# An attention and spectral-mix kernel with some 290 TensorE instructions fewer: the last unit of modes as rows, two batches' last rows side by side, one transpose for v's last keys

## The chip, the cores and the metric

The kernel runs on one core of a Trainium2 chip. The metric is the device time of one execution in microseconds (us), the median of several runs. PE is the matrix engine (TensorE), PEld its weight loads, DVE the vector engine, ACT the scalar engine, POOL the GpSimd engine, which here also issues nearly all loads, and SP the engine that issues the stores. Sixteen DMA engines move the data.

## The reference

```python
def _attn_ref(q, k, v, f):            # 8 batches, 8 heads, 576 rows, 64 columns
    scores = scale * np.matmul(q, k.transpose(0, 1, 3, 2))
    cum = np.cumsum(np.log(np.clip(f, 0.0001, 1.0)), axis=-1)
    decay = cum[:, :, :, None] - cum[:, :, None, :]
    scores = np.where(causal, -1e9, scores + decay)
    attn = np.exp(scores - np.max(scores, axis=-1, keepdims=True))
    attn = attn / (np.sum(attn, axis=-1, keepdims=True) + 1e-09)
    return np.matmul(attn, v)

def _moe_ref(x, w_r, w_i, w_ch):      # x: 8 x 576 x 512; w_r, w_i: 64 x 512 x 512
    X = np.fft.rfft(x, axis=1)
    Y[:, :64] = X[:, :64] times (w_r + 1j * w_i), mode by mode (512 x 512 each)
    u = x + np.fft.irfft(Y, n=S, axis=1)
    return u + np.maximum(u @ w_ch, 0.0)
```

The attention's output, its heads side by side, is the x of the second part. The weights w_r and w_i are 134 MB of float32, read once; they are turned into bf16 on their way in.

## The kernel before, in words

The program is written out in a fixed order for every engine: there is no scheduler.

The attention is a loop of 34 turns over 32 pairs of heads (`pairs`, four head pairs for each of eight batches). Turn i computes the scores and exponentials of pair i (`scores`), the product with v of pair i-1 (`av`, `norm`) and the Fourier modes of pair i-2 (`dft`), and turns q and k of pair i+1 (`trans`). v passes through `scale_v`, `turn_v` (eighteen 64 x 64 transposes into `tv`, then a DVE copy into `vT`) and `back_v` (transposes of vT into `vp`: four of 128 keys, and two of 64 for the last 64 keys, one for each head; then an ACT copy into `vs`). A sequence of 576 rows is five blocks, four of 128 and one of 64 (`SBLK`). At the head of a turn POOL issues the loads of q and k for pair i+4 (L112), of v for pair i+3 (L122), and one or two half tiles of weights (`issue_half`, L167, L176, L185). From turn 10 on, weight tiles that have come in are used at once (`spec_early`).

A weight tile holds a quarter (`dc`, 0 to 3) of a unit `u` of four modes: 1 MB in bf16. There are 16 units, so 64 tiles, in seven buffers and some guests' places. `spec_mms` multiplies a tile as 8 matmuls of 512 columns, the modes of all batches as the small operand; the result is rows of modes in `A`. `spec_cols` does it the other way round, 32 matmuls of 16 columns with the weights as the stationary operand, which gives columns, `AT`, that need no turning. Before the change the last unit (u = 15) is done by `spec_cols` in all its quarters and summed in `accT`. The last tile (15, 3) comes in four pieces, one for each mode.

After the attention, a loop over the units takes the tiles as they come. `Yb` adds the early sums, `to_rows` turns rows into columns (`yps`, into `YT` or `YLa`). Beside this, `xw` multiplies a batch's x by w_ch (XW), and from unit 12 on `folds` adds the first twelve units' modes to x and XW: `fold_modes` once for a batch, then `fold_u` and `fold_z` for each block of rows. `SHARE` sets how much of it lies between two weight tiles; what is left is done ahead of (15, 2). Within (15, 2) and (15, 3) stand `base_mm` calls that start the output's first banks (U0, Z0, U1); those with `stop=True` are repeated later and only keep PE at work.

The tail begins when the last piece is used: six DVE sums put the last modes into `YLa` and `YLw`, `last_modes` turns them, and 18 steps write two blocks of 128 x 512 each (`rest`, `copy_u`, o_sb, out_dram).

## Time and profile before

| | |
|---|---|
| median of 3 runs | 435.96 us (435.72 to 436.53) |
| profiled execution, its own time | 436.07 us |
| its span in the profile | 434.2 us |
| busy, share of the span | PE 83%, DVE 61%, ACT 53%, POOL 32% |
| PE instructions, matmuls and weight loads | 4433 and 4444 |
| moved by DMA | 96.79 MB, 223 GB/s over the span |

The profile is of one execution; times are microseconds from the start of its span. L12 is line 12 of the kernel. A group's row says: line, engine, operation, output from input with its shape, count, busy time, and how long its engine stood idle ahead of it and for what. The page's line GB/s has the span in 40 slices of 10.9 us. In a table of stretches the columns are the stretch, its length, the busy time of PE, PEld, DVE, ACT and POOL with the number of instructions, the granted PE clock, the share of the sixteen DMA engines that is busy (it can pass 1, as packets overlap) and GB/s. The queue q0 carries the loads that POOL issues, q1 SP's transfers, q8 and q14 the engines' instructions.

### The profile page before, as it was taken

The numbers are of one execution on the slowest core, as the hardware profiler recorded it, in microseconds if no ns is written. First come the engines' busy times: TensorE is split into PE (matmuls) and PEld (weight loads), VectorE is DVE, ScalarE is ACT, GpSimd is POOL, SyncE is SP. The second block draws the span as 40 slices with busy tenths as digits, with TensorE's granted clock in tenths as the row PEclk, the third lists the DMA queues.
The fourth block names the chain that finished last, engine by engine and source line by source line (L and its number), as shares of the span: only waits on it lengthen the run. The fifth ranks groups of instructions, "written<-read, shape, count | busy, mean of one in ns | idle before, by whom it ended". The sixth has DMA issues, their size and how long they took to land.

```text
span 434.2 us, 10695 instructions
## 1 busy us (share of the span) xinstructions
PE 360.4 (83%) x4433; PEld 200.9 (46%) x4444; DVE 265.7 (61%) x651; ACT 229.0 (53%) x374; POOL 141.0 (32%) x211
## 2 busy tenths in 40 slices
PE   1699999988898899999986386599788599989993
PEld 1466666655665565665653133244343233334330
DVE  6687888776878797787785122222323157654794
ACT  4656667677775567667661022033313176652783
POOL 6544445434544434444304101111111112001273
PEclk9999999999999999999999579599969699999997
DMA  9999999999999999999999999999999999996598
GB/s 193 205 234 220 232 222 232 226 229 230 231 231 228 230 230 230 230 230 229 236 214 212 212 212 212 212 213 212 212 212 212 212 212 212 211 212 126 188 381 305
DMA packets 60289, 96.79 MB, mean 223 GB/s; under 512 B 3664, under 2 KB 28752, under 8 KB 60240
## 3 DMA queue, kind: packets, MB, share of 16 engines
q0 software_dynamic: 54544, 85.63, 103.6%
q1 hardware_dynamic: 5696, 10.47, 6.7%
q8 instruction: 35, 0.57, 0.5%
q14 instruction: 14, 0.11, 0.1%
HBM read 163.73 MB, written 9.44 MB: 399 GB/s over the span
## 4 chain that ended last, share of the span: by engine, by line
DMA 49%; PE 31%; DVE 9%; ACT 5%; issue 3%; POOL 1%; DVEq 0%; ACTq 0%; POOLq 0%
DMA w<-in_moe_w_i_dram 34%; DMA w<-in_moe_w_r_dram 13%; PE pd L536 5%; PE pav L505 5%; PE sps L457 5%; DVE qkT L382 4%; PE tv L404 3%; ACT et L464 2%; PE A L221 2%; PE pd L557 2%; DVE vT L406 2%; PE tp L377 2%; DMA qk<-in_k_dram 2%; DVE x_all L520 2%; PE U L692 2%
## 5 line engine op out<-in xcount | busy, mean ns | idle before, releaser
L464 ACT ACTIVATE et<-sps 128x1024 bf16<-128x1024 f32 x96 | 93.2, 1023 | 11.6 <-PE sps L457 9.7
L505 PE MATMUL pav<-vs,et 128*128 128x65 bf16 (+1 forms) x896 | 51.3, 197 | 14.6 <-ACT e L451 14.3
L505 PEld LDWEIGHTS <-et 128*128 128x128 bf16 (+1 forms) x896 | 39.9, 103 | 34.0 <-issue 31.7
L382 DVE COPY qkT<-tp 128x640 bf16<-128x640 bf16 x64 | 48.9, 765 | 3.4 <-PE tp L377 3.4
L892 DVE TENSOR_TENSOR Yb<-A,yx 128x512 bf16<-128x512 f32 x15 | 10.4, 692 | 59.0 <-PE A L221 59.0
L406 DVE COPY vT<-tv 128x576 bf16<-128x576 bf16 x32 | 24.2, 757 | 35.4 <-PE tv L404 34.7
L732 PE MATMUL pxw<-wch,xT 128*128 128x512 bf16 (+1 forms) x152 | 41.1, 418 | 1.0 <-DVE xT L722 0.4
L457 PE MATMUL sps<-qkT 64*128 64x512 bf16 (+4 forms) x320 | 39.4, 310 | 1.3 <-DVE qkT L382 1.1
L426 ACT COPY vs<-vp 128x576 bf16<-128x576 bf16 x32 | 20.4, 639 | 37.1 <-PE vp L422 37.1
L520 DVE TENSOR_TENSOR x_all<-pav,rcp 128x384 bf16<-128x384 f32 (+2 forms) x96 | 36.2, 377 | 3.3
L221 PE MATMUL A<-w,XP 128*16 128x512 bf16 (+1 forms) x240 | 21.3, 435 | 20.2 <-DMA w<-in_moe_w_i_dram 12.1
L377 PE MATMUL tp<-ident_bf,qk 128*64 128x128 bf16 x576 | 30.1, 235 | 9.3 <-DMA qk<-in_k_dram 9.0
L185 POOL DMA_DIRECT2D w<-in_moe_w_r_dram x16 | 11.9, 743 | 74.6 <-PE A L221 69.2
L739 ACT CAST XW<-pxw 128x512 bf16<-128x512 f32 (+1 forms) x16 | 9.4, 585 | 45.2 <-PE pxw L732 45.2
L739 ACT CAST yx<-pxw 128x512 bf16<-128x512 f32 (+1 forms) x24 | 14.0, 585 | 33.9 <-PE pxw L732 33.9
L782 ACT CAST x_all<-pu 128x512 bf16<-128x512 f32 (+1 forms) x40 | 23.4, 585 | 13.1 <-PE pu L775 12.2
L112 POOL DMA_DIRECT2D qk<-in_q_dram x32 | 19.5, 609 | 30.8 <-PE tp L377 6.5
L185 POOL DMA_DIRECT2D w<-in_moe_w_i_dram x19 | 13.3, 698 | 50.0 <-PE A L221 40.5
L732 PEld LDWEIGHTS <-xT 128*128 128x128 bf16 (+1 forms) x160 | 15.8, 109 | 22.9 <-issue 9.6
L722 DVE COPY xT<-ptr 128x576 bf16<-128x576 bf16 x32 | 14.7, 458 | 17.8 <-PE ptr L717 17.0
L112 POOL DMA_DIRECT2D qk<-in_k_dram x32 | 19.2, 601 | 19.1 <-DMA w<-in_moe_w_i_dram 5.9
L377 PEld LDWEIGHTS <-qk 128*64 128x64 bf16 x576 | 19.5, 116 | 12.7 <-issue 8.2
(158 smaller groups left out, 703.3 us busy)
## 6 DMA issues: line engine op xcount, KB each, us to landing
w<-in_moe_w_i_dram POOLq DMA_DIRECT2D x19, 1024.0 KB, 31.9
w<-in_moe_w_r_dram POOLq DMA_DIRECT2D x16, 1024.0 KB, 29.9
w<-in_moe_w_r_dram POOLq DMA_DIRECT2D x23, 512.0 KB, 11.3
w<-in_moe_w_i_dram POOLq DMA_DIRECT2D x19, 512.0 KB, 11.0
out_dram<-o_sb SPq DMA_DIRECT2D x36, 256.0 KB, 2.8
vt<-in_v_dram POOLq DMA_DIRECT2D x29, 288.0 KB, 10.4
qk<-in_q_dram POOLq DMA_DIRECT2D x32, 144.0 KB, 10.7
qk<-in_k_dram POOLq DMA_DIRECT2D x32, 144.0 KB, 10.7
```

The lines of the kernel that those rows point to most:

```text
L112: nc.gpsimd.dma_start(qk[64 * n : 64 * n + 64, :, :], src[b, 2 * g : 2 * g + 2, :, :].rearrange("h (p r) d -> p h (r d)", p=64),)
L185: nc.gpsimd.dma_start(w8[:, j : j + step, :, :].rearrange("p m r e -> p m (r e)"), src[m : m + step, 256:512, :].rearrange("m (p r) e -> p ...
L221: nc.tensor.matmul(A[32 * j : 32 * j + M, :], lhsT=lhsT, rhs=rhs, start=st_, stop=sp_)
L377: nc.tensor.transpose(tp[64 * hp : 64 * hp + 64, r - r0, :, :].rearrange("p n c -> p (n c)"), qk[:, hp, r * 64 : r * 64 + 64], ident_bf[:, :],
L382: nc.vector.tensor_copy(st[i]["T"][:].rearrange("p n (c r) -> p n c r", r=9)[:, :, :, r0:r1], tp[:, 0 : r1 - r0, :, :].rearrange("p r n c ...
L406: nc.vector.tensor_copy(st[i]["vT"][:].rearrange("p (c r) -> p c r", r=9), tv[:].rearrange("p r c -> p c r"))
L457: nc.tensor.matmul(ps[:, hp, c : c + n], lhsT=KT[sl, jb * 128 : jb * 128 + 128], rhs=QT[sl, i0 : i0 + n], start=True, stop=True,)
L464: nc.scalar.activation(st[i]["et"][:, T, :, :], ps[:], ACT.Exp, scale=scale)
L505: nc.tensor.matmul(pav[:Ms, sb % 3, hp, :], lhsT=eblk(i, hp, jb, sb), rhs=rhs, start=(jb == 0), stop=(jb == sb),)
L520: nc.vector.tensor_tensor(x_all[:ns, g, b, lo:hi, :].rearrange("p s (h d) -> p s h d", h=2), pav[:ns, lo % 3 : lo % 3 + n, :, 0:Dh], _stri ...
L732: nc.tensor.matmul(pxw[rows, :], lhsT=xT[:, eb, sb * 128 : sb * 128 + Ms], rhs=wch[:, eb, :], start=(eb == 0), stop=(eb == NEB - 1),)
L739: nc.scalar.copy(XW[to][rows, sb, :], pxw[rows, :])
```

## The change

1. The last unit's first three quarters are done by `spec_mms` as rows, as those of the other units are: (15, 0) in the attention, (15, 1) and (15, 2) into one bank A. A float32 sum `Yf` is turned by four float32 matmuls (`ypf`, with `perm_f`) and copied into `accT` between the first and the second piece of the last tile.
2. Z0 is started ahead of (15, 2), U0 between the second and third piece, each once; the repeated `base_mm` calls for U0 and Z0 are gone. U1's stay.
3. The 64 last rows of two batches share one block of 128 partitions of `x_all` (`place`). `xw` treats them as one block for each two batches, and `folds` too.
4. v's last 64 keys are doubled by a POOL copy behind vT, so that one transpose of 128 turns them for both heads; `vs` and `wT` have ten places for nine, and `setup_w` two activations for four.
5. `e4` has one buffer for two. `SHARE` is 19.1 for 19.8.

In the instruction lists PE has 8568 rows for 8862, DVE 643 for 647, ACT 363 for 373, and POOL has 32 copies more.

```diff
@@ turn_v, back_v @@
-        st[i]["vT"] = vTpool.tile([128, S], BF16, tag="vT", name="vT")
+        st[i]["vT"] = vTpool.tile([128, S + 64], BF16, tag="vT", name="vT")
...
+        nc.gpsimd.tensor_copy(st[i]["vT"][:, S : S + 64], st[i]["vT"][:, S - 64 : S])
...
-        for jb in range(4):
+        for jb in range(NSB):
             nc.tensor.transpose(
                 vp[:, 2 * jb : 2 * jb + 2, :].rearrange("p h d -> p (h d)"),
                 vT[:, jb * 128 : jb * 128 + 128],
                 ident_bf[:, :],
             )
-        for hp in range(2):
-            sl = slice(64 * hp, 64 * hp + 64)
-            nc.tensor.transpose(vp[sl, 8, :], vT[sl, 512:576], ident_bf[sl, sl])
@@ spec_early @@
-        if u == NU - 1:
-            AT = psM.tile([128, NEB, 8, B], F32, tag="m", name="AT0")
-            spec_cols(AT, dc)
-            nc.vector.tensor_copy(accT[:], AT[:].rearrange("p e c b -> p e b c"))
-            return
@@ xw @@
+                blocks = [(b, sc) for sc in range(NSB - 1)] + ([(b - 1, NSB - 1)] if b % 2 else [])
...
-                for sb in range(NSB):
+                for to, sb in blocks:
@@ folds @@
+            def modes_to(ps, b, sb, which, start):
+                for c in (b, b + 1) if sb == NSB - 1 else (b,):
+                    rows, _ = place(c, sb)
+                    nc.tensor.matmul(
+                        ps[rows, :],
+                        lhsT=BI[:KF, sb * 128 : sb * 128 + SBLK[sb]],
+                        rhs=ys[c][which][:KF, :],
+                        start=start,
+                        stop=True,
+                    )
...
-            SHARE = 19.8
-            work = [(b, sb) for b in range(B) for sb in range(-1, NSB)]
+            SHARE = 19.1
+            work = [(b, sb) for b in range(B) for sb in range(-1, NSB - 1)]
+            for p in range(B // 2):
+                work.insert(11 * p + 10, (2 * p, NSB - 1))
@@ the last unit @@
                     if last and dc == NEB - 2:
-                        U0 = [bank(psT, "U0") for _ in range(2)]
-                        for n in range(4):
-                            base_mm(U0[n % 2], 0, n % 2, 0, True)
+                        L0 = [bank(psX, "pyl"), bank(psX, "pywl")]
+                        Z0 = [bank(psX, "Z0") for _ in range(2)]
+                        for k in range(2):
+                            base_mm(Z0[k], 0, k, 1)
...
                         if dc < NEB - 1:
-                            spec_cols(AT, dc)
-                            nc.vector.tensor_tensor(
-                                accT[:], AT[:].rearrange("p e c b -> p e b c"), accT[:], ALU.add
-                            )
+                            spec_mms(A, u, dc, dc == 1, dc == 2)
+                            if dc == 2:
+                                Yf = xtp.tile([128, D], F32, tag="yf", name="Yf")
+                                nc.vector.tensor_tensor(Yf[:], A[:], yacc[u // 2][:, u % 2, :], ALU.add)
                         else:
+                            AT = psA.tile([128, NEB, 8, B], F32, tag="a", name="AT1")
                             for j in range(4):
                                 if j == 1:
-                                    for stop in (True, False):
-                                        for k in range(2):
-                                            base_mm(U0[k], 0, k, 0, stop)
+                                    ypf = bank(psT, "ypf")[:, 0 : 64 * NEB].rearrange(
+                                        "p (e c) -> p e c", e=NEB
+                                    )
+                                    for eb in range(NEB):
+                                        nc.tensor.matmul(
+                                            ypf[:, eb, :],
+                                            lhsT=Yf[:, eb * 128 : (eb + 1) * 128],
+                                            rhs=perm_f[:],
+                                            start=True,
+                                            stop=True,
+                                        )
+                                    nc.vector.tensor_copy(
+                                        accT[:], ypf.rearrange("p e (b c) -> p e b c", b=B)
+                                    )
                                 elif j == 2:
-                                    L0 = [bank(psX, "pyl"), bank(psX, "pywl")]
-                                    Z0 = [bank(psX, "Z0") for _ in range(2)]
-                                    for stop in (True, False):
-                                        for k in range(2):
-                                            base_mm(Z0[k], 0, k, 1, stop)
+                                    U0 = [bank(psT, "U0") for _ in range(2)]
+                                    for k in range(2):
+                                        base_mm(U0[k], 0, k, 0)
```

## The prediction

> **What bounds the kernel now.** I read the page first, then the chain that ended last, then the stretch around the last weights, and last the DMA packets themselves. The page:
>
> ```profile
> GB/s 193 205 234 220 232 222 232 226 229 230 231 231 228 230 230 230 230 230 229 236 214 212 212 212 212 212 213 212 212 212 212 212 212 212 211 212 126 188 381 305
> q8 instruction: 35, 0.57, 0.5%
> DMA 49%; PE 31%; DVE 9%; ACT 5%; issue 3%; POOL 1%; DVEq 0%; ACTq 0%; POOLq 0%
> ```
>
> The transfers run at an even 230, then 212 GB/s until slice 36: the weights never stop coming, though PE is at half clock or idle in places. The chain in order of time, from 360 us on:
>
> ```profile
> 375.92 25.61 DMA w<-in_moe_w_i_dram
> 401.58 0.40 PE AT L233 x8
> ```
>
> From 189 us to 401.5 the chain is the weight stream; the rest (401.6 to 434.2) is the tail that computes and writes the output. The timeline around the seam:
>
> ```profile
> 390.55 1.01 PEld L233 LDWEIGHTS <-w 128*128 128x128 bf16 x32 [0.68 <-DMA w<-in_moe_w_i_dram]
> 394.89 1.04 PE L692 MATMUL U<-x_all,ident_il 128*128 128x512 bf16 x4
> 396.56 0.97 PEld L233 LDWEIGHTS <-w 128*128 128x128 bf16 x32 [1.13 <-DMA w<-in_moe_w_r_dram]
> ...
> 401.58 0.28 PEld L233 LDWEIGHTS <-w 128*128 128x128 bf16 x8 [0.65 <-DMA w<-in_moe_w_i_dram]
> ...
> 402.02 0.29 DVE L880 TENSOR_TENSOR YLa<-AT,accT 128x128 bf16<-128x128 f32 x1 [3.91 <-PE AT L233]
> ```
>
> PE waits for every piece of the last unit and starts 0.04 us after it lands. So PE work taken out ahead of 401.5 us gives nothing by itself. But look at the DMA share (last but one column) in the last microseconds of that stream:
>
> ```profile
> 392.00:394.00 2.00, 2.00 (x10) 0.75 (x8) 1.75 (x4) 1.71 (x3) 0.12 (x1) 1.00 1.13 211
> 395.00:396.00 1.00, 0.92 (x4) 0.20 (x2) 0.97 (x2) 0.00 (x0) 0.00 (x0) 1.00 0.68 127
> 398.00:399.00 1.00, 1.00 (x12) 0.35 (x8) 0.11 (x1) 0.00 (x0) 0.00 (x0) 1.00 0.55 102
> 400.00:401.00 1.00, 0.98 (x11) 0.44 (x11) 0.00 (x0) 0.00 (x0) 0.00 (x0) 1.00 0.08 14
> ```
>
> The share falls to a half, then to one engine of sixteen (0.08): the engines don't finish together, and the last one alone holds the kernel. Each transfer leaves sixteen landings in the trace, one per DMA engine. Of the last transfer they stand at 394.48 us (first), six more by 395.8, then 398.3, seven from 398.9 to 399.8, and 401.54. The laggard's distance to the first engine grew in steps: 1.6 us at 25 us, 2.2 at 80, 3.6 at 95, 4.8 at 158, 5.9 at 227, 6.0 still at 384.5 (landings 384.53 to 390.51), 7.1 at 389.5. The steps lie at the packets of queue q8, PE's own instructions (16 KB, 256 instructions, each 0.89 to 1.09 us): numbers 0, 8, 16, 24 and 32 of that queue start at 22.6, 89.4, 155.5, 220.4 and 390.9 us. While one runs, 1.07 fewer data packets are in flight (mean of 30). So these packets go round eight engines, and every eighth stops the laggard for about 1.1 us.
>
> **The change part by part.**
>
> The end of the weights. Number 32, at 390.94 us, is the term. PE had then started 8411 of the trace's 8931 PE records. The instruction lists of the two kernels have 8862 and 8568 rows; four of the added ones are f32 matmuls with a weight load each, so about 290 records go and some 8641 stay. A packet is asked for at a fixed count from the program's start, number 32 near 8384 to 8411 (PE stood at 8384 at its wait before 390.55; number 33, 256 later, came with 8653 started, which gives 8397). In the new program that is 257 to 230 from the end, while the last unit's last weight matmul is 297 from the end, counted in the list. So packet 32 now comes some 40 to 67 PE instructions after the last weight is used, and PE cannot run ahead past its wait for that weight. Number 31 moves to about 388 us, on another engine whose distance (5.3 us) does not lead. The laggard stays at 6.0: last landing 401.54 - 1.06 = 400.48 us. Gain 1.06 us; bounds 0 (the packet still falls ahead) and 1.1.
>
> Is PE ready 1.06 us earlier? The third quarter (15, 2) would land at 395.46 instead of 396.52. Ahead of it: (15, 1) in eight matmuls of 512 columns (0.65 us by the A row, for 1.13), the last folds (12 matmuls for 13; the old ones took 391.5 to 394.95, 0.27 each, so 391.15 to 394.4), the DVE adds that free PSUM for Z0 (1.2 us after PE's last, as before: 395.6) and two Z0 matmuls (0.43): 396.2, so 0.7 us late. Then 0.65 for (15, 2), 0.15 and 0.69 for the DVE sum Yf (the Yb row), four f32 matmuls of 64 columns (0.72 by the cpn row), the second piece (0.40), the DVE copy to accT (0.42), which the second U0 bank waits for, and 0.43 for U0. That ends near 399.6; the third piece and three fillers (0.40, 0.65) bring PE to 400.65, 0.17 us after the last landing. I take 0.15 late; bounds 0 and 0.5. The six deleted filler matmuls (1.04 us at 394.9, 0.4 more later) had lain in waits.
>
> The tail. From the last piece on the list is the same, instruction by instruction, so it shifts whole. One thing changes: packet 34 (422.5 us) puts one engine 1.7 us behind during the output, and its last output still lands at 433.25 where the next engine is 0.4 ahead. The new program is shorter than number 33's count (8640 to 8667, against 8641), so probably no such packet is left: between 0 and -0.55 us, I take -0.3.
>
> The early part. Per turn of the attention loop one transpose fewer (six took 0.60 us, five about 0.5), and (15, 0) in 8 matmuls instead of 32 (0.66 for 1.13): all under the DMA stream, nothing. What is added is a GpSimd copy of 64 columns (the nearest row, YLw 128x192, takes 0.35 us). It stands in GpSimd's queue behind the turn's DMA issues, and PE's back_v waits for it. One turn of before:
>
> ```profile
> 81.94 0.40 PE L415 MATMUL vp<-ident_bf,vT 128*128 128x128 bf16 x4
> ...
> 84.62 0.56 POOL L122 DMA_DIRECT2D vt<-in_v_dram  x1 [2.01 <-DVE vn L394]
> 85.17 0.75 POOL L167 DMA_DIRECT2D w<-in_moe_w_i_dram  x1
> ```
>
> GpSimd would reach this copy at 85.9 us, 4.0 after PE wants it; the same sum is 2.5 at turn 4, 4.0 at turn 9, 4.1 at turn 27. So PE, and DVE behind it, falls 4.3 us back in the attention and stays there, as PE is busy over 85% of it. That is a real new wait, and I cost it at nothing, since PE idles from 237.7 to 241.9 for weights that come at their own pace. GpSimd's issues, in turn, now wait for DVE's vT where PE is the late one: up to 2.6 us at turns 18 to 20, and 5 to 6.5 us at 215 to 229. At those points 1.7 MB, and after the delays 0.9 MB, are still queued: 7.5 and 4.2 us at 225 and 212 GB/s. The stream does not break. If that cover is gone, each microsecond of gap is one of the total.
>
> The rest (setup, one fewer turn of 64 rows per batch pair, 36 for 40 XW matmuls, SHARE) is PE and ACT work under the same stream: nothing.
>
> Two rules of the Trainium skill touch this. The row: PE's clock was halved after windows of 3.4 us with PE busy 0.28 and 0.45 of them, and not after one of 0.53. By "TensorE: Matmul & The Clock Gate" (Part 1) one idle window of about 3.4 us halves the clock, which speaks against taking fillers out. In my schedule PE is busy some 0.75 of 391 to 400.5, so neither row nor rule halves it; it is a rival below. "Runtime: NRT & Kernel Launch" (Instruction fetch mechanics) has blocks of 256 instructions, as the 16 KB packets show, and calls their cost mostly hidden. By that the count of instructions would be worth nothing and the time would stay at 435.9; the landings speak against it.
>
> Sum against the profiled execution (436.07 us, span 434.2): -1.06 + 0.15 - 0.3 = -1.21, so 434.86; the median of the runs is 0.11 lower: **434.8 us**.
>
> **The rivals.**
> - *No gain* (same): packet 32 still meets the laggard, the round goes over other engines, or PE is later than 0.5 us. Against it: the count from the end. For it: the count is known to some 20 instructions and PE's margin is thin. Time 435.5 to 436.0. A halved clock at 397 to 400 us belongs here: the f32 matmuls, pieces and U0 would take about 0.8 us more, 435.6.
> - *GpSimd's queue starves the stream* (slower): copy, vT and issues form one loop. For it: the 4.3 us above. It costs from the point where PE's slip passes 8.7 us (4.3 plus the 4.4 us that 0.9 MB lasts at 212 GB/s); at 11 us the stream stands 2.3 us and the time is 437.1, more at each later turn. Against it: GpSimd idles about 2 us at most issues for a free DMA place, which takes up short delays.
> - *The change does not do what it says*: the lists show 294 PE rows fewer, so no chance for this.
>
> **How the numbers follow.** A measurement of this kernel can tell about 0.2%, 0.87 us. Forecast case 0.60, all of it faster by more than that unless both small terms go wrong; no gain 0.26; starved stream 0.14. The range for 8 in 10: low 434.2 (both small terms at their best, run scatter 0.2), high 436.4 (no gain, plus the 0.5 by which the runs of before scatter upward); the starved stream is left out. The likeliest case alone: 434.2 to 435.2.
>
> **What would show it.** Right: the landings of the last transfer end 6.0 us after the first, the last piece starts near 400.5, q8 has 34 packets or fewer and none between 389 and 400.5; back_v waits for POOL by up to 4 us in the attention; the GB/s line keeps 230 and 212. Wrong: a q8 packet between 390 and 400 with the distance again near 7; the last piece starting well after its landing; or a dip in the GB/s line near 155 or 230 us.

## The result: slower by a quarter of a per cent, and the profile after

The changed kernel takes 436.77 us (median of 17 runs, 435.88 to 437.96) where the kernel before took 435.68 (17 runs, 434.89 to 436.77) on the same chip: 1.0025 times, with a 95% interval of 1.0015 to 1.0035. Forecast was 434.8 (434.2 to 436.4). A second measurement of the same kernel, e5 below, gave 1.0011 [0.9996, 1.0025]. One execution there, a slow one of 545.22 us, is left out of the ratio. The profiled execution took 437.01 us, its span is 435.2 (1.0 more than before).

The lines of its page that answer to those of before:

```profile
GB/s 188 205 235 219 233 220 232 228 226 232 231 230 228 230 229 231 229 231 229 236 214 207 212 212 211 212 212 212 212 212 212 212 212 212 212 211 112 211 382 280
q8 instruction: 34, 0.56, 0.5%
DMA 51%; PE 25%; issue 8%; DVE 6%; POOL 5%; ACT 3%; DVEq 0%; POOLq 0%; ACTq 0%
```

q8 has 34 packets, as forecast. The GB/s line has one small dip, 207 in the 22nd slice (228.5 to 239.4 us). The chain, from 371 us on:

```profile
371.56 28.23 DMA w<-in_moe_w_i_dram
400.26 1.28 PE U L691 x3
401.77 0.85 PE U L691 x2
```

The weight stream still carries it to the tail, but now the chain enters PE through the filler matmuls (U, L691) and not through the last piece of the last weight. The timeline around the seam says why:

```profile
396.05 0.64 PE L221 MATMUL A<-w,XP 128*16 128x512 bf16 x8 [1.11 <-DMA w<-in_moe_w_r_dram]
397.27 0.41 PE L233 MATMUL AT<-XP,w 128*128 128x16 bf16 x8 [0.57 <-DMA w<-in_moe_w_i_dram]
397.52 1.08 PE L849 MATMUL ypf<-perm_f,Yf 128*128 128x64 f32 x8
398.52 0.42 PE L233 MATMUL AT<-XP,w 128*128 128x16 bf16 x8
398.78 0.72 PE L691 MATMUL U<-x_all,ident_il 128*128 128x512 bf16 x2
399.84 0.42 PE L233 MATMUL AT<-XP,w 128*128 128x16 bf16 x8 [0.34 <-DMA w<-in_moe_w_i_dram]
400.10 1.44 PE L691 MATMUL U<-x_all,ident_bf 128*128 128x512 bf16 x3
401.33 0.44 PE L233 MATMUL AT<-XP,w 128*128 128x16 bf16 x8
```

The last transfer's sixteen landings now run from 395.21 to 401.03 us (before: 394.48 to 401.54). The last piece could start at 401.07 and starts at 401.33, behind three fillers that took 1.44 us. The same fillers in the kernel before:

```profile
400.61 0.81 PE L692 MATMUL U<-x_all,ident_bf 128*128 128x512 bf16 x3
401.58 0.40 PE L233 MATMUL AT<-XP,w 128*128 128x16 bf16 x8 [0.16 <-DMA w<-in_moe_w_i_dram]
```

Two windows of the clock, by stretch (the last three columns are granted clock, DMA share, GB/s), first of the changed kernel, then the one that corresponds to it in the kernel before:

```profile
396.36:399.77 3.41, 2.56 (x34) 1.55 (x26) 1.12 (x2) 0.00 (x0) 0.00 (x0) 1.00 0.50 94
399.77:403.18 3.41, 3.22 (x25) 1.70 (x27) 1.01 (x6) 0.09 (x1) 0.00 (x0) 0.50 0.02 4
```

```profile
395.38:398.79 3.41, 2.59 (x47) 1.55 (x45) 1.16 (x3) 0.00 (x0) 0.00 (x0) 1.00 0.60 112
398.79:402.21 3.42, 3.15 (x34) 1.32 (x33) 0.19 (x1) 0.00 (x0) 0.00 (x0) 1.00 0.10 20
```

PE shows the same busy time in the first line of each, 2.56 and 2.59 of 3.41 us, and yet the clock of the next window is 0.50 in one and 1.00 in the other. This pair is the centre of the case. A window of the kernel before with far less busy time, 1.80 us, is followed by one at full clock, too:

```profile
303.21:306.63 3.42, 1.80 (x23) 0.80 (x21) 1.12 (x2) 0.84 (x2) 0.75 (x1) 1.00 1.13 212
306.63:310.04 3.41, 3.27 (x33) 1.83 (x27) 1.83 (x4) 0.05 (x1) 0.74 (x1) 1.00 1.12 212
```

The difference in the spans, in four pieces read from the two traces: the last weight lands 0.51 us earlier (401.03 for 401.54); from that landing to the first output issue it takes 5.12 us instead of 4.31 (+0.81); from there to the last output landing 27.81 instead of 27.40 (+0.41); and from there to the end 1.21 instead of 0.92 (+0.29; over all runs this last step is 0.9 to 1.2 whatever the kernel). Sum +1.00.

The gap in the stream: the first landing of each 1 MB transfer follows the one before by 4.95 us around here, except for one at 236.60, which follows by 5.46, and the next by 5.04. GpSimd's issues there:

```profile
221.87 0.24 POOL L407 COPY vT<-vT 128x64 bf16<-128x64 bf16 x1 [5.33 <-DVE vT L404]
222.36 0.74 POOL L185 DMA_DIRECT2D w<-in_moe_w_r_dram  x1 [0.25 <-issue]
228.44 0.24 POOL L407 COPY vT<-vT 128x64 bf16<-128x64 bf16 x1 [5.34 <-DVE vT L404]
228.92 0.74 POOL L185 DMA_DIRECT2D w<-in_moe_w_i_dram  x1 [0.25 <-PE pav L444]
232.61 0.74 POOL L185 DMA_DIRECT2D w<-in_moe_w_r_dram  x1 [2.95 <-PE A L221]
```

The copy waits 5.3 us for VectorE, and the weight issue behind it, which the kernel before had made at 222.66, is made at 228.92. Its data begin to land at 236.60, 0.5 us later than an unbroken stream would have had them: so long, by the landings, the fastest DMA engine had nothing to move.

### The profile page after: what moved, and what is told of

Its sections match the earlier page's. It is cut to its first block, busy times and chain, and to the rows that moved or that the text cites. A ratio compares the mean times of both kernels' runs of the same rounds, so it can differ in the third digit from the quotient of the medians.

```text
span 435.2 us, 10347 instructions
## 1 busy us (share of the span) xinstructions
PE 343.2 (79%) x4294; PEld 195.8 (45%) x4304; DVE 265.7 (61%) x647; ACT 225.7 (52%) x365; POOL 148.7 (34%) x243
## 4 chain that ended last, share of the span: by engine, by line
DMA 51%; PE 25%; issue 8%; DVE 6%; POOL 5%; ACT 3%; DVEq 0%; POOLq 0%; ACTq 0%
DMA w<-in_moe_w_r_dram 25%; DMA w<-in_moe_w_i_dram 17%; DMA vt<-in_v_dram 3%; PE sps L453 3%; PE pav L506 3%; DMA yx<-in_moe_w_i_dram 3%; PE A L221 3%; PE pd L538 3%; DVE qkT L380 3%; PE pd L559 2%; DMA x_all<-in_moe_w_i_dram 2%; PE U L691 2%; ACT et L460 2%; PE pxw L722 2%; PE Z L691 2%
## 5 line engine op out<-in xcount | busy, mean ns | idle before, releaser
L221 PE MATMUL A<-w,XP 128*16 128x512 bf16 (+1 forms) x248 | 22.8, 446 | 26.9 <-DMA w<-in_moe_w_r_dram 16.0
L422 ACT COPY vs<-vp 128x640 bf16<-128x640 bf16 x32 | 22.3, 697 | 35.2 <-PE vp L414 35.2
L722 PE MATMUL pxw<-wch,xT 128*128 128x512 bf16 x136 | 35.8, 410 | 1.2 <-DVE xT L714 0.8
L729 ACT CAST yx<-pxw 128x512 bf16<-128x512 f32 x22 | 12.9, 586 | 37.6 <-PE pxw L722 37.6
L729 ACT CAST XW<-pxw 128x512 bf16<-128x512 f32 x14 | 8.2, 586 | 39.8 <-PE pxw L722 25.0
L714 DVE COPY xT<-ptr 128x512 bf16<-128x512 bf16 (+1 forms) x32 | 14.0, 456 | 21.6 <-PE ptr L711 20.9
L774 ACT CAST x_all<-pu 128x512 bf16<-128x512 f32 x36 | 20.7, 586 | 11.9 <-PE pu L761 11.2
L392 DVE TENSOR_TENSOR vn<-vt,wn 128x576 bf16<-128x576 f32 x32 | 23.9, 748 | 2.4 <-ACT wn L317 2.4
L538 PE MATMUL pd<-bas,x_all 128*64 128x96 bf16 (+3 forms) x240 | 22.4, 215 | 1.9 <-DVE qkT L380 1.1
```

The source lines that it names most:

```text
L221: nc.tensor.matmul(A[32 * j : 32 * j + M, :], lhsT=lhsT, rhs=rhs, start=st_, stop=sp_)
L392: nc.vector.tensor_tensor(vn[:], st[i]["vt"][:], _strided(wn[:, widx(i), :], [[1, 9], [0, Dh]]), ALU.mult)
L538: nc.tensor.matmul(pd[half, r, :, :] if r else pd[:, 0, :, :], lhsT=xs[:, r - 1 : 128 : 2] if r else xs, rhs=bas3[rows, sc, :, ML:NM] if r ...
L722: nc.tensor.matmul(pxw[:], lhsT=xT[:, eb, sb * 128 : sb * 128 + 128], rhs=wch[:, eb, :], start=(eb == 0), stop=(eb == NEB - 1),)
```

## The experiments

Each was timed in five rounds beside the kernel before on the same chip; the ratio is to that kernel, with its 95% interval (it is taken over all rounds and can differ from the quotient of two medians by 0.001). The landings, steps and clock are from one profiled execution each. "Tail" is the time from the last weight landing to the first output issue, "outputs" from there to the last output landing.

| run | ratio | last weight lands, first to last | tail | outputs | halved clock at the seam |
|---|---|---|---|---|---|
| before | 1 | 394.48 to 401.54 | 4.31 | 27.40 | none |
| after | 1.0025 [1.0015, 1.0035] | 395.21 to 401.03 | 5.12 | 27.81 | 399.8 to 403.2 |
| e5_after_again | 1.0011 [0.9996, 1.0025] | 395.34 to 401.23 | 5.97 | 27.99 | 397.9 to 404.7 |
| e1_copy_on_dve | 0.9987 [0.9969, 1.0004] | 394.56 to 400.19 | 4.85 | 27.91 | 398.3 to 401.8 |
| e14_copy_on_act_alone | 0.9997 [0.9983, 1.0012] | 395.06 to 400.93 | 4.70 | 27.67 | 398.8 to 402.2 |
| e2_fillers | 0.9981 [0.9966, 0.9996] | 394.88 to 400.49 | 4.32 | 27.81 | none |
| e3_both | 0.9982 [0.9968, 0.9997] | 395.41 to 400.69 | 4.32 | 27.87 | none |
| e6_rows_back | 0.9994 [0.9980, 1.0007] | 394.96 to 401.52 | 4.35 | 27.87 | none |
| e7_packet_gone | 0.9992 [0.9969, 1.0014] | 394.55 to 400.06 | 4.33 | 28.05 | none |
| e8_turn_undone | 1.0024 [0.9999, 1.0048] | 394.95 to 401.17 | 8.90 | 27.85 | 396.5 to 406.7 |
| e11_turn_undone_2 | 0.9986 [0.9969, 1.0002] | 394.70 to 400.43 | 4.32 | 27.55 | none |
| e4_before_turn | 0.9992 [0.9973, 1.0011] | 395.62 to 401.91 | 4.32 | 27.39 | none |
| e12_before_no_fillers | 1.0019 [1.0000, 1.0038] | 394.43 to 400.33 | 4.62 | 27.96 | 397.9 to 401.3 |
| e15_before_narrow_fillers | 1.0007 [0.9988, 1.0025] | 394.79 to 402.15 | 4.31 | 27.49 | none |
| e13_narrow_fillers | 0.9989 [0.9973, 1.0005] | 394.37 to 400.32 | 4.33 | 27.68 | none |
| e9_copy_on_act | 0.9971 [0.9955, 0.9987] | 394.94 to 401.02 | 4.32 | 26.79 | none |
| e10_copy_on_dve_bf16 | 0.9976 [0.9962, 0.9991] | 395.22 to 400.97 | 4.31 | 26.62 | none |

The column of the tail sorts the runs at a glance: 4.31 to 4.35 us wherever the clock is not halved, 4.62 to 5.97 where it is halved (8.90 in e8, which has a second fault).

**The copy and the fillers, apart and together.** First the copy moved to VectorE:

```
-        nc.gpsimd.tensor_copy(st[i]["vT"][:, S : S + 64], st[i]["vT"][:, S - 64 : S])
+        nc.vector.tensor_copy(st[i]["vT"][:, S : S + 64], st[i]["vT"][:, S - 64 : S])
```

> The changed kernel with one word changed: VectorE, not GpSimd, copies v's last 64 keys behind vT. Theory (the copy in GpSimd's queue holds each weight issue behind it until DVE's vT is there, and the stream stands 0.5 to 0.7 us at 232 to 236 us): the fastest DMA engine lands its share of the last transfer near 394.5 us instead of 395.21, the last landing is 0.47 us earlier (near 400.5), and the time 0.5 us under the changed kernel's 436.77, 436.3. Rival (the gap has another cause, PE freeing weight buffers later): first landing stays at 395.2 and the time at 436.8.

Measured: no gap, first landing 394.56, last 400.19, as the theory has it. The clock is still halved, after a window in which PE was busy for 2.54 us:

```profile
394.92:398.34 3.42, 2.54 (x34) 1.73 (x33) 1.12 (x2) 0.00 (x0) 0.00 (x0) 1.00 0.69 129
398.34:401.75 3.41, 3.29 (x25) 1.26 (x24) 0.76 (x5) 0.00 (x0) 0.00 (x0) 0.50 0.16 29
```

Yet the median is 435.97 us against 436.17 of the kernel before, so nothing of the loss is left that could be measured.

Then four filler matmuls put back, the copy left on GpSimd:

```
-                            base_mm(Z0[k], 0, k, 1)
+                            base_mm(Z0[k], 0, k, 1, True)
...
+                                if j == 0:
+                                    for k in range(2):
+                                        base_mm(Z0[k], 0, k, 1)
...
-                                    for k in range(2):
-                                        base_mm(U0[k], 0, k, 0)
+                                    for stop in (True, False):
+                                        for k in range(2):
+                                            base_mm(U0[k], 0, k, 0, stop)
```

> The changed kernel with four filler matmuls of 512 columns put back into PE's idle time around the last unit: two (Z0 again) ahead of the first piece of the last quarter, two (U0 again) behind the second piece. Theory (the tail loses 0.8 us because PE's idle time at 396.4 to 399.8 us halves its clock for 399.8 to 403.2): the granted clock stays full to 403, the last piece starts under 0.1 us after its landing instead of 0.30, the first base matmul of the tail comes 2.6 us after the last landing instead of 2.95 (2.1 to 2.2 in the kernel before), and the time is 0.5 to 0.8 us under 436.77: about 436.1. Rival (the clock falls because of the small matmuls, not the idle time): still halved, 436.8. Second rival (the DMA engines set the end whatever PE does in the tail): clock full, time 436.8 all the same.

Measured: 435.74 us against 436.17, and the stretch at the seam keeps its clock:

```profile
394.23:397.64 3.41, 2.10 (x24) 1.28 (x24) 1.39 (x3) 0.00 (x0) 0.00 (x0) 1.00 0.76 142
397.64:401.05 3.41, 3.24 (x37) 1.65 (x36) 0.49 (x2) 0.00 (x0) 0.00 (x0) 1.00 0.28 52
```

Tail 4.32 us, the value of the kernel before. The theory is right for clock and tail. The gain in time has the expected sign: from 1.0025 or 1.0011 to 0.9981 is 0.0030 to 0.0044, or 1.3 to 1.9 us (1.2 to 1.5 by the medians), with ratios that are each known to 0.0010 to 0.0015 only. So it isn't told apart from the 0.5 to 0.8 us expected. Then both edits:

> Both edits, copy on VectorE and fillers back. Theory: the two gains add, 0.5 + 0.6 = 1.1 us under the changed kernel, about 435.6, the time of the kernel before; what is then left against the forecast of 434.8 is the packet of PE's instructions in the output. Rival (the last landing sets nothing, or the clock sets nothing): only one of the two shows.

Measured: full clock, tail 4.32, but a gap again, of 0.79 us at 241.9, although no copy stands in GpSimd's queue. In this execution PE's clock had been halved at 60.4 and at 135.5 us and the last turn of the attention started its vs copy at 231.8 us; in e1 at 230.1. So the copy in GpSimd's queue is not the only thing that opens a gap; an attention that ends late may do it too. In time the rival came out: with 0.9982, the copy on VectorE adds nothing that can be measured to the fillers (0.9981), and the fillers add little to the copy on VectorE (0.9987; 0.2 us by the ratios, 0.5 by the medians). The two gains don't add; either edit alone takes the time back.

**The changed kernel once more, a packet put back, a packet taken out, and the turn undone.** The unaltered kernel, to see which of the three marks come back:

> The changed kernel itself, unaltered, beside the next three. From its first measurement it should take 1.0025 times the kernel before. The terms found in its trace (a gap in the weight stream at 232 to 236 us, a halved clock just ahead of the tail, a packet of PE's instructions in the output) are properties of one execution so far; theory: gap 0.2 to 1.0 us, halved clock in a window between 396 and 404, packet number 33 near 425 all show again. Rival (they are accidents of that execution): the trace shows none or other ones, and the time is 1.000.

Measured: all three do, in an execution that was the slowest of the eleven. The time is 1.0011, with an interval that reaches from 0.9996 to 1.0025, so the loss of the first measurement is not confirmed in size. The gap is 0.29 us, the clock is halved for two windows (397.9 to 404.7, tail 5.97 us), packet 33 is at 426.7. The eleven runs lie between 435.09 and 438.24 us, and the two executions profiled so far have one and two halved windows.

Next, e3 with 270 idle PE instructions, nine in front of each unit's sums:

```
+                        for _ in range(9 if dc == first else 0):
+                            nc.tensor.matmul(
+                                A[0:32, 0:64], lhsT=ident_bf[:, 0:32], rhs=ident_bf[:, 0:64], start=True, stop=True
+                            )
```

> The run with the copy on VectorE and the fillers, plus 270 PE instructions that do nothing of use (nine tiny matmuls ahead of each unit's sums, in time in which PE waits for weights). They move each packet of PE's instructions 270 instructions earlier: number 32 from 403 to about 384 us, inside the weight stream. Theory (packets stop one engine each for 1.06 us, and every eighth the laggard): the lag at the last weight is 6.3 us instead of 5.28, the last landing and the time are 0.8 to 1.06 us later: about 436.4 where the kernel with the copy on VectorE and the fillers took 435.4. Rival (the packets are hidden, the lag has another cause): lag 5.3, time 435.4.

Measured: packet 32 at 383.0 us, and the lag goes from 5.57 us at 370.1 to 6.55 at 390.0 (+0.98). Last landing 401.52 (e3: 400.69). The mechanism is shown for the landing. The time (0.9994, 435.82 us) is 0.4 us above e3's, inside the interval, where 0.8 to 1.06 was expected. PE's clock was granted at 0.95, not 1.00, for most of this execution.

Then 48 PE instructions fewer, by letting VectorE add x in the first 24 folds:

```
+                if xdone[0] <= 24:
+                    modes_to(pu, b, sb, 0, True)
+                    xs = x_all[:, :, b, sb, :]
+                    nc.vector.tensor_tensor(xs, pu[:].rearrange("p (g c) -> p g c", g=NEB), xs, ALU.add)
+                    return
```

> The run with the copy on VectorE and the fillers, with 48 PE instructions fewer: in the first 24 folds VectorE adds x to the modes, where PE did it through the identity. PE's records go from 8659 to 8611, under the 8640 or so at which packet number 33 was asked for. Theory (the end of the program is set by that packet: it stops one engine for 1 us in the output, and the last output lands 1.16 us after its first share): the packet at 424 is gone, the last output's landings are within 0.3 us, the span is 0.7 to 0.9 us shorter and the time about 434.6. Rival (the output is bound by PE and ACT, the lag is hidden behind the end): packet gone, time 435.4. Second rival (the packet comes all the same, since the fetch runs ahead past the end): nothing changes.

Measured: packet 33 is gone (33 packets in all), and still the outputs take 28.05 us. Two other things took its place: the third output issue came 1.56 us after the second (0.71 elsewhere) beside packet 32, now at 404.8 us; and in the last four outputs the last landing is 0.83 to 0.91 us behind the first, after an 8 KB instruction packet of another engine at 426.8. Why these cost so much here was not followed. Time 0.9992 [0.9969, 1.0014]: no gain shown.

Then, with e2's fillers, the fourth part of the change undone, and VectorE adding x in all 36 folds to keep the packets in place:

```
-        for jb in range(NSB):
+        for jb in range(4):
...
+        for hp in range(2):
+            sl = slice(64 * hp, 64 * hp + 64)
+            nc.tensor.transpose(vp[sl, 8, :], vT[sl, 512:576], ident_bf[sl, sl])
```

> The changed kernel with fillers and with its fourth part undone: v's last keys turned by two transposes of 64 rows as in the kernel before, no copy at all; 72 PE instructions are saved in the folds, so the packets stay where they are. Theory (the copy, on either engine, delays PE in the attention, 3.3 to 5 us at its end, and so the last early weight issues): the last turn's vs copy starts at 226.5 to 227.5 us instead of 230.1 to 231.8, no transfer's first landing is more than 5.0 us after the one before, the last transfer's first landing is near 394.5, the time 0.3 to 0.6 us under the run with the copy on VectorE and fillers. Rival (the delay comes from the other parts, the norm of the last 64 rows or spec): the turn ends at 230 all the same.

Measured: the last turn's vs copy starts at 227.3 us (before 226.8), no gap. But the time is 1.0024, by a fault of the experiment: with every fold VectorE was late at the last unit (its fold adds ran to 398.96 us), PE stood, the clock was halved for three windows and the tail took 8.90 us. The profiled execution is the slowest of its twelve (440.81; the median is 436.98). It says nothing on the copy in time. Its repetition with 20 early folds only (`xdone[0] <= 20`):

> The changed kernel with fillers and its fourth part undone (two transposes of 64 rows, no copy), and 20 early folds in which VectorE adds x, so that VectorE is not late at the last unit; packets of PE's instructions come 24 instructions earlier than in the run with copy on VectorE and fillers. Theory: last turn at 226 to 227.5 us, no gap, full clock in the tail, time as with the copy on VectorE and fillers or a little less, 0.997 to 0.998. Rival (the one transpose is worth its copy): 0.999 or more.

Measured: last turn at 224.9, no gap, full clock, tail 4.32, time 0.9986. The attention of e8 and e11 is the same program, so 2.4 us lie between two executions of it. That is no better than e2 and e3, which keep the copy: its worth is not told apart from zero.

**Part four alone, in the kernel before.** turn_v, back_v and wT of the changed kernel, nothing else:

```
+        nc.gpsimd.tensor_copy(st[i]["vT"][:, S : S + 64], st[i]["vT"][:, S - 64 : S])
...
-        for jb in range(4):
+        for jb in range(NSB):
```

> The kernel before with only the fourth part of the change: v's last keys turned by one transpose, with the copy on GpSimd (64 PE instructions fewer over the attention). Theory (the copy starves the stream): copies wait 4 to 5 us for DVE in GpSimd's queue near 215 to 230 us, the fastest engine's last landing comes 0.5 to 0.7 us later than 394.48, and the time is 0.4 to 0.7 us over the kernel before, about 436.2. Rival (the gap of the changed kernel comes from the reordered weight work, not the copy): 435.7. If the 64 fewer instructions move packet 32 off the laggard, the gap shows at the first landing all the same.

Measured: the first landing of the last transfer is 1.14 us later than before (395.62, with a gap of 1.03 at 237.0 and 0.13 at 242.0), so the copy does starve the stream. But the time is 0.9992, as before: the lag of the slowest engine falls by as much (6.38 us at 231.0, 5.21 at 252.0), because the gap stops only the engines that had run ahead. The last landing is 0.37 us later than before, and the lag was already 0.41 larger ahead of the gap (5.97 before).

**Are the fillers the cause? The kernel before without them.**

```
-                        for n in range(4):
-                            base_mm(U0[n % 2], 0, n % 2, 0, True)
...
-                                    for stop in (True, False):
-                                        for k in range(2):
-                                            base_mm(U0[k], 0, k, 0, stop)
+                                    for k in range(2):
+                                        base_mm(U0[k], 0, k, 0)
```

and the same for Z0.

> The kernel before without its eight filler matmuls in the last unit (U0 four times, then U0 and Z0 once each instead of twice); nothing else is changed. Theory (it is the loss of fillers, not the new order of the last unit, that lets the clock fall): the clock is halved in one or two windows of 3.4 us between 395 and 405, the first matmul on the last unit's modes comes 1.4 to 1.8 us after the last landing instead of 0.83, and the time is 0.6 to 1.2 us over the kernel before. Rival (the fillers had lain in waits and did nothing): clock full, time unchanged.

```profile
394.49:397.91 3.42, 1.96 (x43) 1.31 (x42) 1.62 (x3) 0.00 (x1) 0.00 (x0) 1.00 0.65 120
397.91:401.32 3.41, 3.38 (x31) 1.35 (x31) 0.20 (x1) 0.00 (x0) 0.00 (x0) 0.50 0.22 42
```

The clock is halved, and the median is 437.17 us against 435.91: eight matmuls whose results are not used are worth 1.26 us by the medians and 0.8 by the ratio (1.0019, interval from 1.0000), about as much as the whole change costs. The profiled execution happens to be the shortest of its twelve, with one halved window.

**What does the clock go by?** Two runs keep the fillers' time but take seven eighths of the array out of them: a stationary tile of 128x16 instead of 128x128, the same 512 columns streamed. In e3 (they write banks that are still free):

```
+                                if j == 0:
+                                    for k in range(2):
+                                        base_mm(L0[k], 0, k, 1, True, 16)
...
+                                    for k in range(2):
+                                        base_mm(L0[k], 0, k, 0, True, 16)
```

> The run with the copy on VectorE and the fillers, but the four fillers use 16 of the array's 128 columns (a stationary tile of 128x16) and stream the same 512 columns, so they keep PE busy for as long. Rule A (the clock goes by the share of the array's cells at work: counted over the ten traces so far, windows of 3.41 us with under 0.25 of the cells' time in use halved it in 61 of 65 cases, those with over 0.35 in 2 of 807): the four fillers add a tenth of what they added, the window ahead of the tail stays near 0.21 and the clock is halved, time about 0.6 over the run with full fillers, 436.0. Rule B (it goes by the time in which PE is busy): clock full, 435.4.

Measured: full clock, 0.9989. In this execution the windows lay differently, and the share of cells in the one that counts was 0.25, between the two rules. In the kernel before, where all eight fillers are narrowed:

```
-                ps[:],
-                lhsT=ident_bf[:] if sb < last64 else ident_il[:].rearrange("p i j -> p (i j)"),
+                ps[:m, :],
+                lhsT=ident_bf[:, :m] if sb < last64 else ident_il[:].rearrange("p i j -> p (i j)")[:, :m],
```

> The kernel before with its eight fillers kept in place but with a stationary tile of 128x16 instead of 128x128: PE is busy for as long, with an eighth of the array's cells. Rule A (the clock goes by the share of cells at work): as without the fillers, clock halved ahead of the tail and time 1.002 of the kernel before. Rule B (it goes by the time in which PE is busy): as the kernel before, clock full and time 1.000.

```profile
394.89:398.31 3.42, 2.72 (x39) 1.40 (x38) 1.56 (x4) 0.58 (x1) 0.00 (x0) 1.00 0.66 124
398.31:401.72 3.41, 3.29 (x34) 1.50 (x35) 0.41 (x1) 0.00 (x0) 0.00 (x0) 1.00 0.22 41
```

Full clock with about 0.16 of the cells at work, and 1.0007 in time. Rule A is refuted. Busy time as the view shows it (2.72, so 0.80 here) is no rule either: the changed kernel's window with 0.75 was followed by a halved one, and the kernel before's at 303.21 with 0.53 was not. What fits is a third measure, made after these runs: the share of a window in which PE streams columns, that is, sends the columns of the moving operand through the array. Each matmul counts from its start for as long as its moving columns take (512 take 0.213 us, the spacing of matmuls back to back), overlaps once, each recorded f32 pass as twice its columns. So a 16-column piece that the view shows as 0.40 us counts for a few hundredths. (The factor for f32 is a choice: with their columns counted once, the windows that hold them come 0.06 lower.) Over the 17 traces of this case, from some 30 us into the span, about where the traces' records of the clock begin (24 to 34 us), windows of 3.41 us at full clock:

| streaming share | windows | then halved |
|---|---|---|
| under 0.35 | 111 | 109 |
| 0.35 to 0.40 | 27 | 9 |
| over 0.40 | 1582 | 2 |

At half clock, where a column takes twice as long, no window under 0.60 (110 of them) is followed by a full one, and 113 of 118 over 0.70 are: the same number of columns. The window ahead of the tail has 0.33 in the changed kernel, 0.30 in e5, 0.33 in e14 and 0.20 in e12, all halved; 0.40 in the kernel before and 0.43 in e15, not halved. In between the measure doesn't decide: e1 is halved at 0.37 and e8 at 0.40, e6 at 0.37 is not. And e2, e3 and e7 stand at 0.32 to 0.35 with full clock, but in each the trace has the weight load of one more filler and not its matmul, which is 0.06. A filler is 0.0625 of a window. The window at 303.21 has 0.39. Since the measure was chosen after the fact, no experiment here set out to refute it.

**The way out: the copy on ScalarE, fillers, and fewer PE instructions.**

```
-        nc.gpsimd.tensor_copy(st[i]["vT"][:, S : S + 64], st[i]["vT"][:, S - 64 : S])
@@ back_v @@
         vT = st[i]["vT"]
+        nc.scalar.copy(vT[:, S : S + 64], vT[:, S - 64 : S])
```

> The changed kernel with one line moved: the copy of v's last keys is on ScalarE, in back_v; no fillers, folds as they are. Theory (two losses of about equal size: the copy's delay of the attention and of the weight issues, and the halved clock ahead of the tail): the last turn's vs copy starts near 225 us, there is no gap, the clock is halved once between 395 and 405, the time is between the changed kernel (1.0011 to 1.0025 of the kernel before) and the run with copy on ScalarE, fillers and fewer PE instructions (0.9971): about 0.999. Rival (the copy costs nothing in time, all is the clock): as the changed kernel, 1.002.

Measured: last turn at 227.5 us, 2.5 later than expected and 0.7 later than in the kernel before, but 3 earlier than in the changed kernel; no gap, one halved window, tail 4.70, 0.9997. With fillers and 15 folds on VectorE:

> The changed kernel with fillers, with the copy of v's last keys on ScalarE (in back_v, ahead of the transposes), and with 15 folds in which VectorE adds x (30 PE instructions fewer, some 8629 records, so that packet number 33 is not asked for). Theory: the last turn's vs copy starts by 229 us, no gap over 5.0 us between first landings, last weight landing near 400.2, clock full from 350 to 428, 33 packets of PE's instructions, time under the kernel before by 1 us, about 435.0. Rival (ScalarE, which holds the exponentials, falls back in the attention instead): the last turn at 231 or later, and a gap.

```profile
PEclk9999999999999999999998589598898698999998
GB/s 183 205 234 220 228 224 233 223 229 230 232 228 231 228 231 230 229 230 232 230 218 212 212 212 212 212 212 212 212 212 212 212 212 212 212 212 149 176 382 318
```

Measured: last turn at 225.2 us; 434.74 us against 435.91 of the kernel before, 0.9971 [0.9955, 0.9987], the lowest ratio of all, though not told apart from e10, e2 or e3. The GB/s line has no dip, the clock (one digit for each 10.8 us) is full at the seam, and no PE packet falls between 404.5 us and the last output (the 34th, which was not expected, comes at 435.1, after it): the last output's landings end 0.44 us after its first, and the outputs take 26.79 us. A variant with the copy on VectorE, 11 such folds, and

```
-                                Yf = xtp.tile([128, D], F32, tag="yf", name="Yf")
+                                Yf = xtp.tile([128, D], BF16, tag="yf", name="Yf")
...
-                                            rhs=perm_f[:],
+                                            rhs=perm[:],
```

> The same with the copy on VectorE, with the turn of the last unit's rows in bf16 instead of f32 (eight PE records fewer and half the passes), and 11 folds in which VectorE adds x. Theory: first landings without a gap unless the attention ends later than 230.5 us, full clock in the tail, 33 packets, time about 435.0, same as the run with the copy on ScalarE within 0.3. Rival (the f32 passes held the clock up): halved clock ahead of the tail, 435.8.

Measured: 435.02, 0.9976; outputs 26.62 us, last output's landings within 0.28. The clock stays full without f32 passes, so they were not what held it.

## Why the prediction was wrong

Between the two profiled executions the forecast was -1.21 us and the span came out +1.00. The difference of 2.21 has four parts: the landing 0.55 (-0.51 for -1.06), the tail up to the first output issue 0.66 (+0.81 for +0.15), the outputs 0.71 (+0.41 for -0.3) and the last step 0.29, which the forecast didn't have. Step by step, in its own order.

*The end of the weights* (-1.06): right in mechanism, too large. Packet 32 came at 403.3 us, after the last weight; the lag at the end is 5.82 us instead of 7.06. Of the landings, five executions with packet 32 well ahead of the last weight (383 to 392 us, in e4 394.6) end at 401.49 us on average (before, e4, e6, e12, e15), the other twelve at 400.71: 0.8 us. In e12 the packet added only 0.30 us to the lag, since the engine that it stopped was not the last. In the profiled execution it was 0.51.

*PE ready* (+0.15): right for the data and wrong for the clock, and this is the step whose failure the experiments show. (15, 2) started 0.04 us after its landing. But "PE is busy some 0.75 of 391 to 400.5, so neither row nor rule halves it" took the busy column for what the clock goes by. The busy time was indeed 0.75, the streaming share 0.33. The rival priced a halved clock at about 0.8 us for 397 to 400 us; it came in the next window and stretched the tail by 0.81 us (1.66 in e5). So the price was near; what failed was to count it as excluded. Fillers put back brought the full clock and a tail of 4.32 us (e2), and fillers taken out of the kernel before brought the halved clock and 4.62 (e12). The "six deleted filler matmuls", eight by the edit, "had lain in waits": they had, and that was their use.

By "TensorE: Matmul & The Clock Gate" (Part 1) of the Trainium skill, a monitor watches how busy PE is in windows of about 3.4 us and one idle window halves the clock. The windows of 3.41 us and the halved clock of 0.50 agree with every trace here; the full clock is 1.00 in sixteen of the seventeen and 0.95 in e6. What counts as idle in these traces is not only a PE that stands still: by the measure above, windows in which it streams columns for less than about 0.35 lose the clock.

*The tail* (-0.3): wrong sign. The packet came, at 425.6 us. The count was 8641 records against 8640 to 8667, too near to call, and it left something out: each f32 matmul leaves two loads and two matmuls in the trace, so the new program has 8651, and the packet starts with 8631 of them started (8624 to 8650 in the variants of the changed kernel that have it ahead of the end). Outputs +0.41 us; how much of that is the packet's is open, for e12, whose packets come as before, takes 27.96 us. With 8629 records (e9, e10) no such packet comes within the outputs and they take 26.6 to 26.8 us; e7 (28.05) shows that this alone is no promise.

*The early part* (0): the slip of 4.3 us was near (the last turn's vs copy starts at 230.5 for 226.8 us, so 3.7), the cover was not. The queue did hold the 0.9 MB counted: at 228.92 us, 0.93 MB issued had not been moved. But that is 4.4 us as a mean over engines that stand 5 us apart. The fastest had its share of the transfer in hand until 231.14 us, 2.2 us later, and its share of the new one began 2.7 us after the issue, by its landing at 236.60 less 4.95. So the stream broke by 0.2 to 1.2 us in all four traces with the copy on GpSimd (after, e5, e2, e4). But "each microsecond of gap is one of the total" was wrong too: in e4 gaps of 1.16 us in all cost the last landing 0.37 us at most and the time nothing that shows. That need not hold for the changed kernel: there the lag fell by 0.08 us only (5.30 to 5.22) beside a gap of 0.51, with a packet of PE's instructions at 236.09. The worth of the copy lies between nothing (e3 against e2) and 0.6 to 1.7 us by the ratios (e14 and e1 against the two measurements of the changed kernel); the runs don't settle it closer.

The slower rival, GpSimd's queue, did happen. How the loss divides between it and the halved clock stays open: without the copy on GpSimd, e1 takes 0.9987 and e14 0.9997 though their clock is halved, and with fillers e2 takes 0.9981 though its stream still breaks. What is shown is that the deleted fillers let the clock be halved and that this stretches the tail, by 0.81 of the 1.00 us in the profiled pair; the prediction had filed it under "no gain".

By "Runtime: NRT & Kernel Launch" (Instruction fetch mechanics) of the Trainium skill the crossing of a block of 256 instructions is mostly hidden. For the DMA engine that carries the block it is not: e6 shows 0.98 us of lag for one packet. What it costs PE itself was not measured here.

## What to carry to other kernels

Before filler matmuls are taken out of a wait ahead of a tail, count the columns that PE streams in each window of 3.4 us, not its busy time: short matmuls look busy (0.40 us for a piece of eight) and stream little. The measure is a fit to these traces, so try it on a trace of your own. Where all DMA engines must finish, look at each one's last landing and at which instruction packets it carried; a change of a few dozen instructions can move a packet into or out of the end (here 8651 records with it and 8629 without). An operation put on the queue that issues transfers holds up all transfers behind it, so put it on an engine whose queue only computes (here ScalarE, just ahead of its reader). In time, that move alone was not told apart from the kernel before (0.9997).

## What the runs showed of the hardware that was not expected

The clock does not go by how much of the array is in use: fillers of 16 of 128 columns held it as well as full ones (about 0.16 of the cells at work, clock 1.00). A gap in a DMA stream can stop only the engines that run ahead and leave the slowest one its backlog: in e4 it shortened the spread (6.38 to 5.21 us) more than it delayed the end. And a matmul of 64 f32 columns leaves two loads and two matmuls in the trace: four of them took 1.08 us at full clock and 1.95 at half (e8).
